# An attention and mixture-of-experts kernel on one core: the products with v of a half of the queries in one run, and their copies out of PSUM later in the order

## The chip, the cores and the metric

The kernel runs on one core of a Trainium2 chip. The metric is the device time of one launch in microseconds; lower is better. The core has five engines with an instruction stream each: TensorE (PE in the profile; PEld is its weight loads), VectorE (DVE), ScalarE (ACT), GpSimd (POOL) and SyncE (SP), which here only issues DMAs.

## The reference, cut to what matters

```python
scores = scale * np.matmul(q, k.transpose(0, 1, 3, 2))      # 8 batches, 8 heads, 576 x 64
scores = scores + bias.transpose(2, 0, 1)[None, :, :, :]    # a small MLP of the positions
scores = scores - np.max(scores, axis=-1, keepdims=True)
attn = np.exp(scores)
attn = attn / (np.sum(attn, axis=-1, keepdims=True) + 1e-09)
x = np.matmul(attn, v)                                      # then to tokens x 512
...
e_idx = np.argmax(x @ w_gate + modality_bias[modality_id], axis=1)
out[mask] = gate_w[mask, None] * (relu(x[mask] @ w1[e]) @ w2[e])   # for each of 8 experts
```

Everything is float32. The output has 4608 rows of 512.

## The kernel before

The program has three stages: a table of position biases, attention, and the experts. The change lies in attention, in the function `attention`.

Attention works on two heads of one batch at a time, a pair; there are 32 pairs, n = 0 to 31. The 576 queries of a pair come in five chunks (four of 128 for each head and a last one of 64 for both heads together), so a pair has nine score slots. A round of the outer loop over n has five steps u = 0 to 4, and the table `ORDER` says for each step, in letters, what is issued in which order. Every engine takes its own instructions in the order in which the letters issue them, so the table alone sets the order on each engine. The letters that matter:

- S: `scores`, four matmuls (line 420) into one of two score buffers `sps`; then VectorE adds the bias, takes the minimum and writes the chunk to `Eb` (line 435). e and f: ScalarE's exp (line 449) of the step's first and second score slot.
- t and T: `etrans`, four transposes of an exp chunk for head 0 and head 1 into PSUM, `eps[0]` for t and `eps[1]` for T (line 463), and a copy to `eT`. For the last chunk, in step u = 1, t is line 469 and T is the narrow transpose of line 474 (64 output columns for each head) into `eps[1]`, whose copy goes to `rT`. `take` is the copy out of PSUM; the list `ON_ACT` names those that ScalarE does (line 309), the others VectorE does. The transposes of chunk 3 of the round before (step 0) are both copied by ScalarE.
- R: `rtrans`, which transposes what is left of four chunks (line 491) into `rT`.
- a, A, b, c: `av`, the products with v of the pair before, n - 1. Half 0 of the queries is a and then A, half 1 is b and then c. Each letter is four narrow products (line 507, 64 output columns for each head, two heads side by side); A and c end with a product over all 128 columns (line 517). The float32 products are each run in two passes, so the profile counts eight for a letter. A and c then copy the sum out of PSUM to `xTb` on ScalarE (`av0`, `av1`).
- 0 to 4: `prep`, transposes of the next pair's q and k (lines 369 and 374) and their copies to `QT` and `KT`; there are prep steps for 30 of the rounds that have products.
- X and B are steps of the routing, W and K issue DMAs that swap halves of `QT` and gather `KH` and `QD` for the next pair's scores, C copies a remainder on GpSimd (line 454).

Three kinds of PSUM tile matter: `sps`, `eps`, and the two banks `xps`, handed out in turn by `xbank` to R, X, prep and the products. Whoever gets a bank waits until the copy out of its last use is done. In the listings, `xps_77` and `xps_78` are these two banks, `eps_751` and `eps_752` are `eps[0]` and `eps[1]`, `sps_749` and `sps_750` the two score buffers.

Of the kernel before, what the change touches and what calls it, by code (L numbers as in the profile page):

```python
# [22 lines left out]
S = 576  # L23
# [5 lines left out]
HS = S // 2  # L29
# [76 lines left out]
class Attn:  # L106
# [151 lines left out]
    def attn_early(self, st, rst):  # L258

        tc, nc, io = self.tc, self.nc, self.io  # L260
        pool = lambda **kw: st.enter_context(tc.tile_pool(**kw))
        cp = pool(name="ac", bufs=1)
        self.raw = pool(name="raw", bufs=2)
        self.Eb = cp.tile([P, 4, 2, S], F32, name="Eb")
        self.e_next = itertools.cycle(range(4))
        self.xrb = [cp.tile([P, XW], F32, name=f"xrb{k}") for k in range(2)]
        self.xr_next = itertools.cycle(self.xrb)
        right = lambda **kw: rst.enter_context(tc.tile_pool(side="right", **kw))

        last = (self.B - 1) % 2  # L270
        xp = {last: right(name="xtp_last", bufs=1), 1 - last: cp}
        self.xTb = [xp[k].tile([P, NP, S], F32, name=f"xTb{k}") for k in range(2)]
        self.smp = right(name="smp", bufs=2)
        self.rt = right(name="rt", bufs=1)

        self.idr = cp.tile([P, P], F32R, name="idr")
        nc.scalar.copy(self.idr, self.idf)
        self.eT = cp.tile([P, 2, 4, S], F32, name="eT")
        self.rT = cp.tile([P, S], F32, name="rT")
        self.qs = cp.tile([P, 9, 2, D], F32R, name="qs")  # L280
        self.ks = cp.tile([P, 9, 2, D], F32R, name="ks")
        self.KT = [cp.tile([P, 2, S], F32R, name=f"KT{k}") for k in range(2)]
        self.KH = cp.tile([P, S], F32R, name="KH")
        self.QD = cp.tile([P, P], F32R, name="QD")
        nc.gpsimd.memset(self.QD.bitcast(F32), 0.0)
        self.vrem = []
        for k in range(2):
            nc.vector.memset(self.QT[k][:, 0, 576:640].bitcast(F32), 0.0)
            vr = cp.tile([P, P], F32, name=f"vrem{k}")
            nc.vector.memset(vr, 0.0)  # L290
            self.vrem.append(vr)
        self.qraw, self.kraw, self.vmain, self.E, self.rem, self.sums, self.xT = {}, {}, {}, {}, {}, {}, {}

    def attn_late(self, st):

        pp = st.enter_context(self.tc.tile_pool(name="aps", bufs=1, space=PSUM))
        self.sps = [pp.tile([P, 2, 512], F32, name=f"sps{k}") for k in range(2)]
        self.eps = [pp.tile([P, 4, P], F32, name=f"eps{k}") for k in range(2)]
# [195 lines left out]
    def av(self, n, half, part):  # L494

        nc = self.nc
        if half == 0 and part == 0:
            self.xT[n] = self.xTb[n // NP % 2][:, n % NP, :]
        if part == 0:
            self.avps = self.xbank()  # L500
        v = self.vmain[n]
        sl = slice(HS * half, HS * half + HS)
        ps = self.avps[:, 0:HS]
        for k in (0, 1) if part == 0 else (2, 3):
            for h in range(2):
                o = slice(64 * h, 64 * h + 64)
                nc.tensor.matmul(  # L507
                    ps[o, :],
                    v[:, h, k, :],
                    self.eT[:, h, k, sl],  # L510
                    start=k == 0,
                    stop=False,
                    tile_position=(0, 64 * h),
                    skip_group_check=True,
                )
        if part == 1:
            nc.tensor.matmul(ps, self.vrem[n % 2], self.rT[:, sl], start=False, stop=True, skip_group_check=True)  # L517
        if part == 1:
            self.take(f"av{half}", self.xT[n][:, sl], ps)
            if half == 1:  # L520
                del self.vmain[n]

    def first_steps(self, route):

# [31 lines left out]


    ORDER = (
# [5 lines left out]
    )  # L564

    def attention(self):
        n_pair = self.n_pair
        tail = self.first_tiles() if self.K else {}
        for u, k in self.LATE:
            tail.setdefault((0, u), []).append(lambda k=k: next(self.late[k], None))  # L570
        bg = None
        for n in range(n_pair + 1):
            for u in range(5):
                for f in tail.get((n, u), ()):
                    f()
                if u == 4 and n > 0 and n % NP == 0:
                    assert not bg or all(k == len(x) for x, k in bg)
                    bg = self.route_steps(n // NP - 1)
                m, w = (n, u - 2) if u >= 2 else (n - 1, u + 3)
                scored = []  # L580
                for op in self.ORDER[u].split():
                    if op in "SefC":
                        if n == n_pair:
                            continue
                        if op == "S":
                            scored.append(self.scores(n, 2 * u + len(scored)))
                        elif op == "C":
                            self.compact(n, u)
                        else:
                            self.exps(*scored["ef".index(op)])  # L590
                    elif op in "tT":
                        if 0 <= m < n_pair:
                            self.etrans(m, w, "tT".index(op))
                    elif op in "RaAbc":
                        if n > 0:
                            self.rtrans(n - 1) if op == "R" else self.av(n - 1, *divmod("aAbc".index(op), 2))
                    elif op in "k01234WKV":
                        if n + 1 < n_pair:
                            if op in "01234":
                                self.prep(n + 1, int(op))()  # L600
                            else:
                                {"k": lambda: self.split(n + 1, 1), "W": lambda: self.swap(n + 1), "K": lambda: self.heads(n + 1), "V": lambda: self.load_v(n + 1)}[op]()
                    elif op in "qL":
                        if n + 2 < n_pair:
                            self.split(n + 2, 0) if op == "q" else self.load_qk(n + 2)
                    elif f := self.route_next(bg, "XB".index(op)):
                        f()
                if 0 <= m < n_pair:
                    del self.E[m, w]
        self.bg = bg  # L610
# [817 lines left out]
```

## Time and profile before

| what | value |
|---|---|
| median of three runs | 1195.97 us (1191.96 to 1196.64) |
| the profiled execution, its time | 1198.66 us |
| its span from the first to the last instruction | 1196.7 us |
| mean granted TensorE clock | 0.983 |
| TensorE matmul busy | 1132.1 us, 95% of the span |
| VectorE, ScalarE, GpSimd busy | 754.1, 728.3, 383.7 us (63%, 61%, 32%) |

All times below are of the profiled execution, which lies 2.7 us above the median of the runs. A row of the timeline has the start, the length from the start of its first to the end of its last instruction, the engine, line, operation, the tiles, and how many instructions it merges. A matmul's row ends after its results are out, so rows of neighbouring groups overlap; what a group costs TensorE is the distance from its start to the next group's start.

### The profile page before, as it was taken

Reading aid. Unit: us, or ns where it says so; the run is one execution under the profiler, and the core shown is the slowest. Engines: PE = TensorE matmul, PEld = TensorE weight load, DVE = VectorE, ACT = ScalarE, POOL = GpSimd, SP = SyncE. Lnnn points to the kernel's source line nnn. Section 1 sums busy time; section 2 is a strip of 40 time slices with the busy share of each in tenths; the row PEclk is TensorE's granted clock in tenths of the full one; section 3 lists DMA queues with packets and bytes.
Section 4 is the critical chain, followed back from the end, with each engine's and each line's share of the span. In section 5 each row is a group of like instructions: output and inputs, shape, how many; then the busy total and the mean of one; then the engine's idle time right before and its main releaser. Section 6 shows DMA issues by size and latency. Waiting matters only on the chain. (4 is left out here: it accounts for less than half of the span.)

```text
span 1196.7 us, 23090 instructions
## 1 busy us (share of the span) xinstructions
PE 1132.1 (95%) x8202; PEld 919.5 (77%) x8202; DVE 754.1 (63%) x1552; ACT 728.3 (61%) x1412; POOL 383.7 (32%) x525
## 2 busy tenths in 40 slices
PE   7977999899999899999998979999999999999997
PEld 3445777667778577777776758988899899989975
DVE  7974567457666475666757637577555645664667
ACT  5565667657767477677775654545545645554566
POOL 2203223434435325444353323532221123122122
PEclk9998999999999999999999999999999999999999
DMA  6854433764745635555365560221113314311361
GB/s 173 192 121 126 112 95 102 115 94 111 125 96 126 98 93 125 113 121 125 93 116 111 162 108 10 72 67 37 45 55 115 107 45 144 113 45 48 121 244 33
DMA packets 91311, 124.26 MB, mean 104 GB/s; under 512 B 35697, under 2 KB 60657, under 8 KB 91188
## 3 DMA queue, kind: packets, MB, share of 16 engines
q1 hardware_dynamic: 83188, 101.35, 36.3%
q0 software_dynamic: 8000, 21.35, 5.9%
q8 instruction: 68, 1.11, 0.5%
q14 instruction: 55, 0.45, 0.1%
HBM read 140.09 MB, written 19.90 MB: 134 GB/s over the span
## 5 line engine op out<-in xcount | busy, mean ns | idle before, releaser
L435 DVE CUSTOM_DVE_ANT_0 Eb<-sps,NBm 128x576 f32<-128x576 f32 x256 | 190.1, 755 | 183.8 <-PE sps L420 93.7
L449 ACT ACTIVATE Eb<-Eb,mn 128x576 f32<-128x576 f32 x288 | 221.5, 770 | 40.5 <-DVE mn L435 36.7
L420 PE MATMUL sps<-KT,QT 128*128 128x288 f32 x1152 | 222.7, 319 | 22.0 <-DMA QT<-QT 21.1
L420 PEld LDWEIGHTS sps<-KT,QT 128*128 128x128 f32 x1152 | 166.5, 191 | 27.4 <-issue 22.3
L1144 PE MATMUL p<-QT,w1hi 128*128 128x256 f32 x1152 | 163.9, 285 | 5.2 <-ACT w1hi L1117 5.2
L463 PE MATMUL eps<-idf,Eb 128*128 128x128 f32 x1024 | 159.9, 282 | 0.6 <-DVE lgs L781 0.3
L507 PE MATMUL xps<-eT,vraw 128*64 128x288 f32 x1024 | 155.0, 425 | 1.5 <-DVE QT L1129 1.0
L1144 PEld LDWEIGHTS p<-QT,w1hi 128*128 128x128 f32 x1152 | 150.8, 194 | 7.3 <-ACT w1hi L1117 6.1
L463 PEld LDWEIGHTS eps<-idf,Eb 128*128 128x128 f32 x1024 | 114.9, 142 | 39.5 <-issue 29.5
L1170 POOL DMA_INDIRECT out<-mo,idt x36 | 51.8, 1440 | 291.1 <-ACT mo L1169 262.6
L1147 DVE SCALAR_TENSOR_TENSOR hl<-p,hh 128x512 fp32r<-128x512 f32 x72 | 49.7, 690 | 138.9 <-ACT hh L1146 134.6
L454 POOL COPY rem<-Eb 128x128 f32<-128x128 f32 x128 | 37.5, 297 | 252.3 <-ACT Eb L449 245.1
L309 ACT ACTIVATE eT<-eps 128x512 f32<-128x512 f32 x192 | 111.4, 591 | 9.5 <-PE eps L463 8.7
L1161 PE MATMUL p<-w2lo,hh 128*128 128x512 f32 x288 | 112.9, 392 | 3.5 <-DVE w2lo L1111 2.2
L1111 DVE TENSOR_TENSOR w2lo<-NBm,w2hi 128x1024 fp32r<-128x1024 f32 x81 | 98.7, 1224 | 24.9 <-ACT w2hi L1110 24.8
L1161 PE MATMUL p<-w2hi,hh 128*128 128x512 f32 x288 | 114.0, 396 | 0.0
L1161 PE MATMUL p<-w2hi,hl 128*128 128x512 f32 x288 | 112.5, 391 | 0.0
L1146 ACT ACTIVATE hh<-p 128x512 fp32r<-128x512 f32 x72 | 43.1, 598 | 111.2 <-PE p L1144 103.1
L309 ACT ACTIVATE xTb<-xps 128x288 f32<-128x288 f32 x64 | 26.4, 412 | 122.9 <-PE xps L517 118.8
L507 PEld LDWEIGHTS xps<-eT,vraw 128*64 128x64 f32 x1024 | 63.1, 138 | 46.6 <-issue 12.6
L1111 DVE TENSOR_TENSOR w1lo<-NBm,w1hi 128x1024 fp32r<-128x1024 f32 x84 | 97.9, 1227 | 0.0
L1144 PE MATMUL p<-QT,w1lo 128*128 128x256 f32 x576 | 93.4, 285 | 0.3 <-DVE w1lo L1118 0.3
(227 smaller groups left out, 1991.3 us busy)
## 6 DMA issues: line engine op xcount, KB each, us to landing
NBm<-moe_w SPq DMA_DIRECT2D x24, 2048.0 KB
NBm<-moe_w SPq DMA_DIRECT2D x46, 1024.0 KB
QT<-QT SPq DMA_DIRECT2D x64, 304.0 KB
NBm<-xTb SPq DMA_DIRECT2D x32, 288.0 KB
KH<-KT SPq DMA_DIRECT2D x64, 144.0 KB
qraw<-q SPq DMA_DIRECT2D x32, 256.0 KB
kraw<-k SPq DMA_DIRECT2D x32, 256.0 KB
vraw<-v SPq DMA_DIRECT2D x32, 256.0 KB
```

The lines of the kernel that those rows point to most:

```text
L309: self.nc.scalar.activation(out, ps, AF.Copy, scale=scale)
L420: nc.tensor.matmul(ps[:, half, :], q, k[:, HS * half : HS * half + HS], start=i == 0, stop=i == len(terms) - 1, skip_group_check=True,)
L435: nc.vector.tensor_tensor_reduce(out=e.rearrange("p (t w) -> p t w", t=2), in0=ps, in1=nb.rearrange("p (t w) -> p t w", t=2), scale=1.0, s ...
L449: self.nc.scalar.activation(e, e, AF.Exp, bias=mn, scale=-1.0, accum_out=sm)
L463: nc.tensor.transpose(ps[:, k, :], e[:, part, P * k : P * k + P], self.idf)
L507: nc.tensor.matmul(ps[o, :], v[:, h, k, :], self.eT[:, h, k, sl], start=k == 0, stop=False, tile_position=(0, 64 * h), skip_group_check=True,)
L1111: (lo or self.nc.vector).tensor_tensor(l, w, h.bitcast(F32), op=ALU.subtract)
L1144: nc.tensor.matmul(ps[:, a, :], w[:, c, fs], x[:, c, :], start=i == 0, stop=i == len(ops) - 1)
L1146: nc.scalar.activation(hh[:, sl, :], ps, AF.Relu)
L1147: nc.vector.scalar_tensor_tensor(hl[:, sl, :], ps, 0.0, hh[:, sl, :].bitcast(F32), op0=ALU.max, op1=ALU.subtract)
L1161: nc.tensor.matmul(ps, h[:, f, sl], m[:, f, :], start=i == 0, stop=i == len(ops) - 1)
L1170: nc.gpsimd.indirect_dma_start(out=self.out, out_offset=IndirectOffsetOnAxis(ap=ids, axis=0), in_=o, in_offset=None, bounds_check=self.n_t ...
```

## The change

The four letters a, A, b, c move, two letters y and z are new, and the narrow transpose T of step 1 moves. The products of half 0 are issued as one run in step 1, directly behind the narrow transposes; those of half 1 as one run in step 3. The copies out of PSUM are split from the products (`av_out`, letters y and z) and are issued behind the step's second score and a transpose. Each half has its own entry in `avps`, so that the copy finds its bank.

```diff
+        self.avps = [None, None]
...
-            self.avps = self.xbank()
+            self.avps[half] = self.xbank()
...
-        if part == 1:
-            self.take(f"av{half}", self.xT[n][:, sl], ps)
-            if half == 1:
-                del self.vmain[n]
+
+    def av_out(self, n, half):
+        self.take(f"av{half}", self.xT[n][:, HS * half : HS * half + HS], self.avps[half][:, 0:HS])
+        if half == 1:
+            del self.vmain[n]
...
-        "S R S e f k X T a t B C",
-        "L S 1 A t e S 4 f 0 C T",
-        "t S S e f b q C T",
-        "B S c e S T 3 2 t f W C V",
+        "S R S e f k X T t B C",
+        "L S 1 T e a A S t y 4 f 0 C",
+        "t S S e f q C T",
+        "B S e b c S T z 3 2 t f W C V",
...
+                    elif op in "yz":
+                        if n > 0:
+                            self.av_out(n - 1, "yz".index(op))
```

The lines behind these shift by a few: 420 becomes 421, 463 becomes 464, 507 becomes 508, 309 becomes 310 and so on. A narrow group counted as x4 here is eight matmuls in the profile.

On TensorE, steps 0 and 1 of round 3, from the first products with v on, before:

```order
L507 MATMUL xps_78<-eT,vraw_1153 64x288 x4
L463 MATMUL eps_751<-idf,Eb 128x128 x4
L420 MATMUL sps_749<-KT_109,QT_73 128x288 x4
L369 MATMUL xps_77<-idr,qs 128x128 x4
L507 MATMUL xps_78<-eT,vraw_1153 64x288 x4
L517 MATMUL xps_78<-rT,vrem_114 128x288
L469 MATMUL eps_751<-idf,Eb 128x128 x4
L420 MATMUL sps_750<-KT_109,QT_73 128x288 x4
L374 MATMUL xps_78<-idr,qs 128x128
L374 MATMUL xps_78<-idr,ks 128x128
L369 MATMUL xps_77<-idr,qs 128x128 x4
L474 MATMUL eps_752<-idf,Eb 64x64 x2
```

and in the changed kernel, from the transposes T of step 0 on:

```order
L464 MATMUL eps_752<-idf,Eb 128x128 x4
L464 MATMUL eps_751<-idf,Eb 128x128 x4
L421 MATMUL sps_749<-KT_109,QT_73 128x288 x4
L370 MATMUL xps_78<-idr,qs 128x128 x4
L475 MATMUL eps_752<-idf,Eb 64x64 x2
L508 MATMUL xps_77<-eT,vraw_1153 64x288 x8
L518 MATMUL xps_77<-rT,vrem_114 128x288
L421 MATMUL sps_750<-KT_109,QT_73 128x288 x4
L470 MATMUL eps_751<-idf,Eb 128x128 x4
L375 MATMUL xps_78<-idr,qs 128x128
L375 MATMUL xps_78<-idr,ks 128x128
L370 MATMUL xps_77<-idr,qs 128x128 x4
```

The two groups of products of half 0 are one group of eight and stand right behind the narrow transposes (now 475), which have moved ahead of the second score; between the end of these products (518) and the transposes of q into the same bank `xps_77` stand a score group, four transposes and two more.

On TensorE, steps 2 and 3 of the same round, before:

```order
L420 MATMUL sps_749<-KT_109,QT_73 128x288 x4
L420 MATMUL sps_750<-KT_109,QT_73 128x288 x4
L507 MATMUL xps_78<-eT,vraw_1153 64x288 x4
L463 MATMUL eps_752<-idf,Eb 128x128 x4
L420 MATMUL sps_749<-KT_109,QT_73 128x288 x4
L507 MATMUL xps_78<-eT,vraw_1153 64x288 x4
L517 MATMUL xps_78<-rT,vrem_114 128x288
L420 MATMUL sps_750<-KT_109,QT_73 128x288 x4
L463 MATMUL eps_752<-idf,Eb 128x128 x4
L369 MATMUL xps_77<-idr,ks 128x128 x4
L369 MATMUL xps_78<-idr,ks 128x128 x4
```

and now:

```order
L421 MATMUL sps_749<-KT_109,QT_73 128x288 x4
L421 MATMUL sps_750<-KT_109,QT_73 128x288 x4
L464 MATMUL eps_752<-idf,Eb 128x128 x4
L421 MATMUL sps_749<-KT_109,QT_73 128x288 x4
L508 MATMUL xps_78<-eT,vraw_1153 64x288 x8
L518 MATMUL xps_78<-rT,vrem_114 128x288
L421 MATMUL sps_750<-KT_109,QT_73 128x288 x4
L464 MATMUL eps_752<-idf,Eb 128x128 x4
L370 MATMUL xps_77<-idr,ks 128x128 x4
L370 MATMUL xps_78<-idr,ks 128x128 x4
```

The products of half 1 are one group too. The bank that they write, `xps_78`, is wanted again by the last row, as before.

On ScalarE, steps 1 to 3 of the same round, before, from the copy of half 0 on (`xTb` is the copy out of the products, `KT` that of a prep step, `rT<-eps` that of the narrow transposes, `Eb` an exp):

```order
L309 ACTIVATE xTb_94<-xps_78 128x288
L309 ACTIVATE eT<-eps_751 128x4x2x64
L449 ACTIVATE Eb,sums_1377<-Eb,mn_2_1423 128x576
L309 ACTIVATE KT_108<-xps_78 128x2x64
L449 ACTIVATE Eb,sums_1377<-Eb,mn_3_1446 128x576
L309 ACTIVATE rT<-eps_752 128x64
L309 ACTIVATE eT<-eps_751 128x4x128
L449 ACTIVATE Eb,sums_1377<-Eb,mn_4_1472 128x576
L449 ACTIVATE Eb,sums_1377<-Eb,mn_5_1478 128x576
L309 ACTIVATE xTb_94<-xps_78 128x288
L449 ACTIVATE Eb,sums_1377<-Eb,mn_6_1499 128x576
L309 ACTIVATE eT<-eps_752 128x4x128
```

and now:

```order
L310 ACTIVATE rT<-eps_752 128x64
L450 ACTIVATE Eb,sums_1377<-Eb,mn_2_1419 128x576
L310 ACTIVATE eT<-eps_751 128x4x2x64
L310 ACTIVATE xTb_94<-xps_77 128x288
L310 ACTIVATE KT_108<-xps_78 128x2x64
L450 ACTIVATE Eb,sums_1377<-Eb,mn_3_1443 128x576
L310 ACTIVATE eT<-eps_751 128x4x128
L450 ACTIVATE Eb,sums_1377<-Eb,mn_4_1472 128x576
L450 ACTIVATE Eb,sums_1377<-Eb,mn_5_1478 128x576
L450 ACTIVATE Eb,sums_1377<-Eb,mn_6_1495 128x576
L310 ACTIVATE eT<-eps_752 128x4x128
L310 ACTIVATE xTb_94<-xps_78 128x288
```

The copy `xTb` of half 0 stood ahead of the copy `eT` of step 1 and an exp, and now stands behind both; that of half 1 stood ahead of an exp and the copy `eT` of step 3, and now stands behind both.

More of the change, by code (lines that the diff above doesn't have):

```diff
@@ L499, in av @@
         if part == 0:
-            self.avps = self.xbank()
+            self.avps[half] = self.xbank()
         v = self.vmain[n]
         sl = slice(HS * half, HS * half + HS)
-        ps = self.avps[:, 0:HS]
+        ps = self.avps[half][:, 0:HS]
         for k in (0, 1) if part == 0 else (2, 3):
```

## The prediction

> **What bounds the kernel now.** I read the page first, then a table of stretches (the span cut at the start and the end of the rounds that hold products, and one undisturbed round), then who waits for whom, then the timeline of TensorE and of ScalarE in that round.
>
> ```profile
> PE 1132.1 (95%) x8202; PEld 919.5 (77%) x8202; DVE 754.1 (63%) x1552; ACT 728.3 (61%) x1412; POOL 383.7 (32%) x525
> ...
> 98.26:712.36 614.10, 592.60 (x4569) 461.65 (x4569) 380.76 (x1021) 411.64 (x979) 236.56 (x382) 0.98 0.53 112
> 468.31:486.83 18.52, 18.52 (x146) 14.02 (x145) 11.57 (x31) 13.06 (x33) 9.58 (x15) 1.00 0.67 128
> ```
>
> The columns of the last two rows are the stretch, its length, and the busy time of TensorE, weight loads, VectorE, ScalarE and GpSimd, then the clock. In the undisturbed round TensorE is busy for all of its 18.52 us; ScalarE has 5.5 us free, VectorE 7. So whatever shortens TensorE's row of groups shortens the round, and whatever makes TensorE wait for another engine lengthens it, as long as the others keep up. In the whole stretch TensorE waits for 21.5 us, most of it outside the change:
>
> ```profile
> PE sps L420 <- DMA QT<-QT: 21.1, 4, 13.9
> ...
> PE xps L374 <- POOL ks L356: 4.2, 2, 3.0
> ...
> PE xps L491 <- POOL rem L454: 3.6, 1, 3.6
> ```
>
> (The 13.9 us are before the stretch.) Here is TensorE's row of groups in the undisturbed round, from T of step 0 to t of step 3:
>
> ```profile
> 469.27 0.60 PE L463 MATMUL eps<-idf,Eb 128*128 128x128 f32 x4
> 469.80 1.19 PE L507 MATMUL xps<-eT,vraw 128*64 128x288 f32 x8
> 470.92 0.66 PE L463 MATMUL eps<-idf,Eb 128*128 128x128 f32 x4
> 471.33 0.78 PE L420 MATMUL sps<-KT,QT 128*128 128x288 f32 x4
> 471.95 0.45 PE L369 MATMUL xps<-idr,qs 128*128 128x128 f32 x4
> 472.33 1.19 PE L507 MATMUL xps<-eT,vraw 128*64 128x288 f32 x8
> 473.45 0.75 PE L517 MATMUL xps<-rT,vrem 128*128 128x288 f32 x2
> 474.04 0.60 PE L469 MATMUL eps<-idf,Eb 128*128 128x128 f32 x4
> 474.39 0.78 PE L420 MATMUL sps<-KT,QT 128*128 128x288 f32 x4
> 475.01 0.22 PE L374 MATMUL xps<-idr,qs 128*128 128x128 f32 x1
> ...
> 475.13 0.50 PE L369 MATMUL xps<-idr,qs 128*128 128x128 f32 x4
> 475.56 0.34 PE L474 MATMUL eps<-idf,Eb 128*64 128x64 f32 x4
> 475.83 0.66 PE L463 MATMUL eps<-idf,Eb 128*128 128x128 f32 x4
> 476.24 1.30 PE L420 MATMUL sps<-KT,QT 128*128 128x288 f32 x8
> 477.47 1.19 PE L507 MATMUL xps<-eT,vraw 128*64 128x288 f32 x8
> 478.59 0.66 PE L463 MATMUL eps<-idf,Eb 128*128 128x128 f32 x4
> 479.01 0.77 PE L420 MATMUL sps<-KT,QT 128*128 128x288 f32 x4
> 479.71 1.19 PE L507 MATMUL xps<-eT,vraw 128*64 128x288 f32 x8
> 480.83 0.75 PE L517 MATMUL xps<-rT,vrem 128*128 128x288 f32 x2
> 481.21 0.91 PE L420 MATMUL sps<-KT,QT 128*128 128x288 f32 x4
> 481.95 0.60 PE L463 MATMUL eps<-idf,Eb 128*128 128x128 f32 x4
> 482.31 0.89 PE L369 MATMUL xps<-idr,ks 128*128 128x128 f32 x8
> 483.02 0.63 PE L463 MATMUL eps<-idf,Eb 128*128 128x128 f32 x4
> ```
>
> And ScalarE in the same round, with one row of the weight loads and one of VectorE:
>
> ```profile
> 470.10 0.39 PEld L507 LDWEIGHTS xps<-eT,vraw 128*64 128x64 f32 x4
> ...
> 470.33 0.78 ACT L449 ACTIVATE Eb<-Eb,mn 128x576 f32<-128x576 f32 x1
> ...
> 471.11 1.11 ACT L309 ACTIVATE eT<-eps 128x512 f32<-128x512 f32 x2
> ...
> 473.45 0.30 PEld L517 LDWEIGHTS xps<-rT,vrem 128*128 128x128 f32 x2 [0.44 <-issue]
> ...
> 474.24 0.41 ACT L309 ACTIVATE xTb<-xps 128x288 f32<-128x288 f32 x1 [2.02 <-PE xps L517]
> ...
> 474.68 0.60 ACT L309 ACTIVATE eT<-eps 128x512 f32<-128x512 f32 x1
> ...
> 477.15 0.76 DVE L435 CUSTOM_DVE_ANT_0 Eb<-sps,NBm 128x576 f32<-128x576 f32 x1 [0.37 <-issue]
> ...
> 482.69 0.59 ACT L309 ACTIVATE eT<-eps 128x512 f32<-128x512 f32 x1
> ...
> 483.23 0.60 ACT L309 ACTIVATE KT<-xps 128x512 fp32r<-128x512 f32 x1
> ```
>
> **What the change takes from TensorE.** No matmul goes or comes; what goes is borders between narrow and full-width groups (the 0.44 us in which the weight loads stand still at 473.45 is part of one). A run of eight narrow matmuls costs 1.12 us with its borders (469.80 to 470.92). Inside it, the last four loads, 0.14 us each (page: 138 ns), take 0.39 us, so two side-by-side matmuls follow the last two after 0.25 us, a little less without the step between the heads; I take 0.24. Sixteen in one run then cost 1.12 + 4 x 0.24 = 2.08 us in place of 2.24, and the groups beside them lose their own borders.
>
> First stretch, T of step 0 to t of step 2: 475.83 - 469.27 = 6.56 us before. After: T 0.44 and t 0.36 (transposes as at 481.95, 0.36, and one more step of 0.08 between two such groups), scores 0.62, prep 0.38, narrow transposes 0.20, products 2.08, line 517 0.38 (as at 480.83), scores behind it 0.74 (as at 481.21), t 0.36, then 0.20 for the two and 0.36 for the four prep transposes (eight take 0.71 at 482.31). The sum is 6.12: 0.44 us less.
>
> Second stretch, scores of step 2 to the second score of step 3: 481.21 - 476.24 = 4.97 before. After: eight scores 1.15 (0.62 for four, and the x8 row is 0.52 longer than an x4 row), T 0.36, scores 0.70, products 2.08, line 517 0.38, in all 4.67: 0.30 less. Together 0.74 us a round; 32 runs of products: **24 us less**.
>
> The trace has no narrow transposes directly ahead of narrow products. If that border were free, the group would cost 0.11 (two steps of its own); if it cost as leaving and entering do now, 0.27 (475.56 to 475.83) and some 0.1 more: 0.2 is nearer to what stays in one shape; the ends are 3 us less and 5 us more over all rounds. [...]
>
> **What the change makes TensorE wait for.** Three places, in the same round's times.
>
> T of step 1 writes `eps[1]`, which holds chunk 3's transposes until ScalarE has copied them. That copy stands behind the exp of step 0's second score (470.33), which nothing in the change moves: the pair of copies begins at 471.11, the first is out at about 471.70 (591 ns on the page). The new row reaches T at 469.27 + 0.44 + 0.36 + 0.62 + 0.38 = 471.07. Wait: **0.63 us**. Behind it stand all products. Rounds with a step X have one more copy ahead of it on ScalarE and four more transposes on TensorE, which nearly cancel. Before, T came 4.5 us later and nothing waited.
>
> Prep 0 takes the bank that half 0's products filled. ScalarE copies it only behind `eT` of step 1, which itself needs t. From the first transpose of t, the row at 474.04 is finished 0.60 later, the copy starts 0.04 after that (474.68), the next copy follows 0.54 after a first (482.69 to 483.23) and takes 0.41: the bank is free 1.59 us after t began. TensorE is at prep 0 after 0.36 + 0.20 = 0.56. Wait: 1.03, with about 0.02 for the signal **1.05 us**. Behind it stand t and all of step 2. Before, the copy went first (474.24 to 474.65) and its bank was asked for at 475.01.
>
> Prep 2 takes the bank of half 1 in the same way: T, `eT` and the copy end 1.59 after T began; T and prep 3 take 0.36 + 0.36 = 0.72. Wait: **0.88 us**.
>
> A small one: step 3's first score needs the buffer that VectorE empties in 0.76 us (477.15). With step 2 shortened by one run of products it comes about **0.1 us** early.
>
> The exp moved ahead on ScalarE gains nothing, since ScalarE had 2.02 us free there (474.24) and does not set the end. GpSimd and SP keep their order; the swap's DMAs depend on prep 0's copy, which comes 1.2 us later, while the round grows by more.
>
> **The sum.** 30 rounds x (1.05 + 0.88) = 57.9; 31 x (0.63 + 0.1) = 22.6; less 24: +56.5 us. Against that, some waits that are there now shrink when TensorE comes later: those in the first fence but for the 13.9, 15 us (7.2 + 4.2 + 3.6), and some half-speed clock behind the long ones. They hang on DMAs and on GpSimd's own pace, and each round leaves them 0.6 to 1.9 us more. Bounds 0 and 15; I take 9. Result +47: 1198.66 + 47 = 1246 for a profiled execution, and 2.7 less, **1243 us**, for the median.
>
> **Rivals.**
> 1. Faster. The waits do not bind, only the borders go: 1196 - 24 = 1172. [...] It decides if ScalarE has emptied a half's bank within 0.56 us of t's start, against 1.59 by the rows. That needs the copy ahead of `eT`, and the listing has it behind. [...]
> 2. Smaller loss: the wait at T is hidden (23 us less) or the old waits go whole (6 less), about 1220.
> 3. Larger loss: prep 0 and 2 come so late that the swap and the gather reach the next pair's scores late more often; the three such waits of the first fence now cost 7.2 us together, up to 3 each, and one in every second round at 1.5 us gives 22 more: about 1265.
> 4. A wash, if the waits are half of what I count: within 6 us of before.
>
> **Chances.** Forecast (1228 to 1256) 0.70; smaller loss 0.12; larger 0.11; faster 0.04; wash 0.03. The range 1216 to 1264 leaves out the faster and the wash cases and the outer part of the rest. About 0.5% is what a measurement of this kernel can tell: slower by more than that 0.93, within it 0.03, faster 0.04.
>
> **What would show it.** Right: in the changed trace TensorE waits on ScalarE at the narrow transposes, at the four prep 0 transposes and at prep 2's, some 30 times each, of 0.6, 1.0 and 0.9 us; a plain round is 20.2 to 20.6 us long; TensorE's busy share in attention falls to about 88%; the two runs of products start eight narrow passes 0.24 us apart. Wrong: no wait at the prep transposes, or copies of the products that start ahead of `eT`'s end. The prediction fails if the borders are worth much more than 0.74 us a round, or the bank is free earlier than the row of copies says.

## The result, and the profile after

The changed kernel is slower: 1253.53 us median against 1194.47 for the kernel before on the same chip, a ratio of 1.0498 (95% interval 1.0467 to 1.0528), so 59 us more where 47 were forecast (range 1216 to 1264). The profiled execution of the changed kernel took 1256.16 us, its span 1254.2.

The stretches of the changed kernel: all rounds with products, then the four rounds of one batch; ahead of them the same four rounds of the kernel before (the third, 18.52 us, is the undisturbed round of the prediction). Columns as in the prediction, with the share of the DMA engines' time and the GB/s that they moved at the end.

```profile
430.49:449.61 19.12, 18.79 (x149) 14.78 (x148) 14.82 (x47) 13.98 (x35) 5.48 (x11) 1.00 0.35 90
449.61:468.31 18.70, 18.70 (x151) 15.20 (x150) 10.77 (x25) 13.58 (x32) 10.41 (x15) 1.00 0.63 142
...
486.83:505.17 18.34, 18.34 (x151) 14.59 (x150) 11.50 (x30) 12.38 (x31) 6.98 (x14) 1.00 0.43 103
```

```profile
98.40:769.75 671.35, 586.63 (x4568) 469.37 (x4566) 380.05 (x1021) 413.54 (x979) 237.03 (x382) 0.99 0.47 103
...
459.91:481.85 21.94, 18.92 (x148) 15.08 (x147) 14.91 (x47) 14.19 (x35) 5.50 (x11) 1.00 0.31 79
481.85:502.60 20.75, 18.54 (x151) 15.46 (x150) 10.80 (x25) 13.68 (x32) 10.41 (x15) 1.00 0.51 128
502.60:523.14 20.54, 18.37 (x147) 14.28 (x146) 11.53 (x31) 13.12 (x33) 9.31 (x15) 1.00 0.64 118
523.14:543.11 19.97, 18.21 (x152) 14.80 (x151) 11.37 (x29) 12.36 (x31) 7.21 (x15) 1.00 0.41 91
```

A round that kept TensorE busy throughout now has two microseconds in which it does nothing: 20.54 us with 18.37 busy, in place of 18.52 with 18.52. TensorE's busy share of the stretch fell from 96% to 87%, while its busy time fell by only 6 us, though the saved borders are worth about 25 (below): the profile counts a part of each new wait, in which the last results still come out, as busy. In the plain round the four waits come to 2.82 us (below), and TensorE's idle time to 2.17. The other engines' busy times are nearly the same, so nothing became a new bound by its load. Who waited for whom on TensorE:

```profile
PE xps L370 <- ACT xTb L310: 45.3, 58, 0.9
PE eps L475 <- ACT eT L310: 19.6, 29, 1.1
```

These are the three places of the forecast with its counts: the prep transposes (two places in a round, 58 times in all) behind the copy `xTb` of the products, and the narrow transposes behind the copy `eT`. The plain round, TensorE and then ScalarE, with one row of VectorE at the end:

```profile
504.97 0.45 PE L370 MATMUL xps<-idr,qs 128*128 128x128 f32 x4
506.03 0.34 PE L475 MATMUL eps<-idf,Eb 128*64 128x64 f32 x4 [0.61 <-ACT eT L310]
506.19 2.11 PE L508 MATMUL xps<-eT,vraw 128*64 128x288 f32 x16
508.24 0.75 PE L518 MATMUL xps<-rT,vrem 128*128 128x288 f32 x2
...
509.36 0.60 PE L470 MATMUL eps<-idf,Eb 128*128 128x128 f32 x4
509.71 0.30 PE L375 MATMUL xps<-idr,qs 128*128 128x128 f32 x1
509.85 0.23 PE L375 MATMUL xps<-idr,ks 128*128 128x128 f32 x1
510.94 0.54 PE L370 MATMUL xps<-idr,qs 128*128 128x128 f32 x4 [0.86 <-ACT xTb L310]
...
512.84 0.60 PE L464 MATMUL eps<-idf,Eb 128*128 128x128 f32 x4
513.43 0.80 PE L421 MATMUL sps<-KT,QT 128*128 128x288 f32 x4
...
517.73 0.54 PE L370 MATMUL xps<-idr,ks 128*128 128x128 f32 x4
518.97 0.28 PE L370 MATMUL xps<-idr,ks 128*128 128x128 f32 x1 [0.70 <-ACT xTb L310]
```

```profile
505.40 1.06 ACT L310 ACTIVATE eT<-eps 128x512 f32<-128x512 f32 x2
...
509.99 0.60 ACT L310 ACTIVATE eT<-eps 128x512 f32<-128x512 f32 x1 [2.60 <-PE eps L470]
510.49 0.41 ACT L310 ACTIVATE xTb<-xps 128x288 f32<-128x288 f32 x1
...
518.01 0.60 ACT L310 ACTIVATE eT<-eps 128x512 f32<-128x512 f32 x1 [1.72 <-PE eps L464]
518.51 0.41 ACT L310 ACTIVATE xTb<-xps 128x288 f32<-128x288 f32 x1
...
512.61 0.76 DVE L436 CUSTOM_DVE_ANT_0 Eb<-sps,NBm 128x576 f32<-128x576 f32 x1 [0.33 <-POOL rem L455]
```

At 506.03 the narrow transposes start 0.05 us after the first copy of the pair at 505.40 is out (0.58 long, to 505.98). At 509.99 ScalarE, which had stood idle for 2.60 us, copies `eT` first; the products' copy ends at 510.90, and the prep transposes begin 0.04 later. TensorE's second half of the round repeats this: the copy at 518.51 ends at 518.92, and the transposes begin at 518.97. The number in brackets counts from the end of the last result; from the moment TensorE could have gone on, the waits are 0.68 (506.03 less 504.97 and 0.38), 1.03 (510.94 less 509.71 and 0.20) and 0.88 us (518.97 less 517.73 and 0.36). A fourth wait shows no bracket: the score at 513.43 starts 0.59 us behind the transposes at 512.84, which alone take 0.36; VectorE's row at 512.61 reads its buffer until 513.37.

### The profile page after: what moved, and what is told of

It is laid out like the page before. It is cut to its first block, busy times and chain, and to the rows that moved or that the text cites. A ratio compares the mean times of both kernels' runs of the same rounds, so it can differ in the third digit from the quotient of the medians.

```text
span 1254.2 us, 23070 instructions
## 1 busy us (share of the span) xinstructions
PE 1125.0 (90%) x8202; PEld 927.0 (74%) x8202; DVE 753.7 (60%) x1552; ACT 729.8 (58%) x1412; POOL 386.3 (31%) x525
## 4 chain that ended last, share of the span: by engine, by line
PE 54%; DMA 13%; issue 11%; ACT 9%; DVE 6%; POOL 5%; SPq 3%; POOLq 0%; ACTq 0%; DVEq 0%
PE p L1149 12%; PE p L1166 12%; PE xps L508 7%; PE sps L421 7%; PE eps L464 4%; ACT Eb L450 4%; PE bps L187 3%; DMA NBr<-xg,idt 3%; DMA qraw<-q 3%; PE xps L518 2%; ACT eT L310 2%; PE xps L370 2%; DMA xg<-xrb 2%; DMA QT<-QT 2%; ACT xTb L310 1%
## 5 line engine op out<-in xcount | busy, mean ns | idle before, releaser
L421 PE MATMUL sps<-KT,QT 128*128 128x288 f32 x1152 | 227.8, 324 | 22.9 <-DMA QT<-QT 16.9
L421 PEld LDWEIGHTS sps<-KT,QT 128*128 128x128 f32 x1152 | 169.2, 192 | 39.7 <-issue 17.8
L464 PE MATMUL eps<-idf,Eb 128*128 128x128 f32 x1024 | 149.5, 277 | 1.2 <-ACT eT L310 0.7
L508 PE MATMUL xps<-eT,vraw 128*64 128x288 f32 x1024 | 139.1, 415 | 0.7 <-issue 0.7
L464 PEld LDWEIGHTS eps<-idf,Eb 128*128 128x128 f32 x1024 | 117.5, 142 | 9.6 <-DVE mn L436 5.0
L508 PEld LDWEIGHTS xps<-eT,vraw 128*64 128x64 f32 x1024 | 69.0, 139 | 45.2 <-issue 7.9
L1116 DVE TENSOR_TENSOR w1lo<-NBm,w1hi 128x1024 fp32r<-128x1024 f32 x84 | 97.9, 1228 | 0.3 <-ACT w1hi L1115 0.3
L1115 ACT CAST w2hi<-NBm 128x1024 fp32r<-128x1024 f32 x84 | 86.8, 1041 | 0.9 <-PEq L1280 0.9
```

What stands on the lines that cost most here:

```text
L421: nc.tensor.matmul(ps[:, half, :], q, k[:, HS * half : HS * half + HS], start=i == 0, stop=i == len(terms) - 1, skip_group_check=True,)
L464: nc.tensor.transpose(ps[:, k, :], e[:, part, P * k : P * k + P], self.idf)
L508: nc.tensor.matmul(ps[o, :], v[:, h, k, :], self.eT[:, h, k, sl], start=k == 0, stop=False, tile_position=(0, 64 * h), skip_group_check=True,)
L1115: self.nc.scalar.copy(h, w)
L1116: (lo or self.nc.vector).tensor_tensor(l, w, h.bitcast(F32), op=ALU.subtract)
```

## The experiments

Each is given as the change of `ORDER` (the lines with a minus say of which kernel), and as a ratio to the kernel before, run on the same chip. Where two profiles are compared, they can be from different chips. The changed kernel itself ran once more, on a second chip:

> The changed kernel as it is, beside these on one chip. All theories: ratio to before 1.045 to 1.053, as the first time.

Measured: 1265.18 us against 1205.08, ratio 1.0498 (1.0462 to 1.0534), as on the first chip.

Theory: the time lies in TensorE's waits for ScalarE's copies. Rivals: the long narrow runs themselves, or the moved narrow transposes alone.

**Copies directly behind the products.**

```diff
-        "L S 1 T e a A S t y 4 f 0 C",
+        "L S 1 T e a A y S t 4 f 0 C",
-        "B S e b c S T z 3 2 t f W C V",
+        "B S e b c z S T 3 2 t f W C V",
```

> The changed kernel with both copies of the products issued directly behind the products, ahead of the score and the transpose; the merged runs and the early narrow transposes stay. Theory (TensorE waits for the bank at prep 0 and prep 2): those two waits go, 30 x (1.05 + 0.88) = 58 us, some 5 us of the old waits on DMAs and GpSimd come back: about 1200 us (1195 to 1206); a plain round 18.6 us in place of 20.5; the wait at the narrow transposes stays at 0.6 to 1.0 us, 30 times. Rival (the merged runs or the moved narrow transposes are what costs): 1240 or more, and TensorE still stands 40 us elsewhere.

Measured: ratio 1.0125 (1.0078 to 1.0173). Three quarters of the loss went with the place of the two copies, and the waits at prep with it; the narrow transposes still wait (21.2 us in 28 waits). So the rival is out as the main cost. But the kernel is some 9 us above the forecast, outside its range, and its plain round is 19.01 us, not 18.6. One wait is new, the first transposes of step 2 behind `eT`; and step 3's first score waits as in the changed kernel:

```profile
564.60 0.34 PE L475 MATMUL eps<-idf,Eb 128*64 128x64 f32 x4 [0.61 <-ACT eT L310]
...
569.22 0.66 PE L464 MATMUL eps<-idf,Eb 128*128 128x128 f32 x4 [0.22 <-ACT eT L310]
...
570.78 0.60 PE L464 MATMUL eps<-idf,Eb 128*128 128x128 f32 x4
571.36 0.80 PE L421 MATMUL sps<-KT,QT 128*128 128x288 f32 x4
```

**Narrow transposes back at the end of step 1**, copies late.

```diff
-        "L S 1 T e a A S t y 4 f 0 C",
+        "L S 1 e a A S t y 4 f 0 C T",
```

> The changed kernel with the narrow transposes back at the end of step 1, the merged runs and the late copies kept. Theory: the wait at the narrow transposes goes (31 x 0.65, in one round of four 1.0: 22 us), their own two borders come back (about 0.25 us a round, 8 us), the waits at prep 0 and prep 2 stay: about 1239 us (1232 to 1245). Rival (the early narrow transposes are the main cost): below 1215.

Measured: ratio 1.0342 (1.0293 to 1.0392), 41 us above before (by this chip's times; 44 were expected). The waits at prep are what they were (45.7 us in 59). So the narrow transposes' early place costs about 19 us of the 60, net of the border that it saves, and the late copies most of the rest.

**The copies moved alone**, products in four runs as before.

```diff
-        "L S 1 A t e S 4 f 0 C T",
+        "L S 1 A t e S y 4 f 0 C T",
-        "B S c e S T 3 2 t f W C V",
+        "B S c e S T z 3 2 t f W C V",
```

> The kernel before with only the copies moved: the products stay in four runs, the copy of half 0 is issued behind t, the exp and the second score, that of half 1 behind the score and T. Theory: prep 4 now waits for half 0's bank, which is free after eT, an exp and the copy, about 1.4 us later than asked for, and prep 2 waits 0.88 us: 30 x 2.3 = 68 us, less up to 10 of old waits: about 1257 us (1245 to 1265). Rival (late copies cost nothing by themselves, only with the merged runs): 1195 us.

Measured: ratio 1.0447 (1.0395 to 1.0499), 51 us, where some 62 were expected. Late copies cost this much without any merged run:

```profile
PE xps L375 <- ACT xTb L310: 36.4, 30, 1.2
PE xps L370 <- ACT xTb L310: 20.8, 30, 0.7
```

**Everything that gains, nothing that waits?** The narrow transposes stand between the two halves of the run.

```diff
-        "L S 1 T e a A S t y 4 f 0 C",
+        "L S 1 e a T A y S t 4 f 0 C",
-        "B S e b c S T z 3 2 t f W C V",
+        "B S e b c z S T 3 2 t f W C V",
```

> The merged runs with the copies directly behind the products, and the narrow transposes between the first and the second half of the products of half 0, so that their PSUM tile has one microsecond more to come free. Theory: no new wait but 0.2 us at step 3's first score; the borders gain 0.74 us a round, 24 us, less 6 for that score and up to 5 of old waits that grow: about 1179 us (1172 to 1186), ratio to before 0.98 to 0.993. Rival (fewer borders gain nothing, TensorE meets another wait): 1192 or more.

Measured: ratio 1.0028 (1.0003 to 1.0053). A miss: no gain. The borders are gone, yet a plain round takes 18.32 us:

```profile
550.34:568.66 18.32, 18.10 (x146) 14.22 (x145) 11.43 (x31) 13.28 (x33) 9.56 (x15) 1.00 0.62 133
```

```profile
557.70 0.66 PE L464 MATMUL eps<-idf,Eb 128*128 128x128 f32 x4 [0.22 <-ACT eT L310]
558.12 1.31 PE L421 MATMUL sps<-KT,QT 128*128 128x288 f32 x8
559.26 0.60 PE L464 MATMUL eps<-idf,Eb 128*128 128x128 f32 x4
559.85 0.79 PE L421 MATMUL sps<-KT,QT 128*128 128x288 f32 x4
```

The groups that moved away had filled two latencies. The transposes at 557.70 now follow so soon that `eT` of step 1 is not out: between the two transposes stood a score and the narrow transposes. And from T at 559.26 to the score at 559.85 it takes 0.59 us where T alone takes 0.36, since the score's buffer is not empty: VectorE's row at 559.02 takes 0.76 us and reads it until 559.78. Before, the first products of half 1 stood ahead of T. The second shows in the changed kernel as well (512.84 to 513.43 is 0.59). The first does not: there the prep transposes wait for a copy that comes after `eT`, and step 2's transposes follow them without a wait.

**One score ahead of those transposes.** The kernel of the last run, with

```diff
-        "t S S e f q C T",
+        "S t S e f q C T",
```

> The run before it (narrow transposes inside the merged run, copies directly behind the products), with step 2's first score moved ahead of its first transposes: S t S in place of t S S. That run's plain round lost 0.22 us to those transposes, which waited for ScalarE's copy of step 1's, and 0.23 us to step 3's first score, which waited for VectorE. Theory (the moved products had covered these two waits, and the saved borders went there): both go, since the score fills the first and reaches VectorE 0.4 us earlier; a plain round takes 17.8 to 17.95 us in place of 18.33, 30 x 0.45 = 13 us, of which up to 6 are lost to old waits on DMAs and GpSimd that grow: ratio to before 0.985 to 0.996. Rival (the saved borders never existed): a plain round of 18.3 us and a ratio of 1.00 or more.

> The same kernel as the run with step 2's score ahead, beside the one with the earlier loads on one chip: ratio to before 0.990 to 0.997, as the first time.

Measured: ratio 0.9935 (0.9906 to 0.9964), and in the repetition on another chip 0.9979 (0.9958 to 1.0000), outside what was expected of it. The round has no wait, and is a little shorter than forecast (17.8 to 17.95):

```profile
542.52:560.23 17.71, 17.71 (x146) 14.21 (x145) 11.44 (x31) 12.60 (x30) 7.31 (x10) 1.00 0.69 132
```

So the borders are worth 18.52 - 17.71 = 0.81 us a round. Of the 25 us that this makes over 31 rounds, 2.5 to 8 us arrive. The profile shows more of the waits on other chains:

```profile
PE sps L421 <- DMA QT<-QT: 24.8, 9, 14.0
PE p L1149 <- DVE w1lo L1123: 11.8, 2, 11.0
PE xps L375 <- POOL ks L357: 10.8, 4, 6.2
PE xps L492 <- POOL rem L455: 5.2, 5, 2.1
```

Scores wait 10.8 us for the swap of `QT` (beside the first 14.0), where it was 7.2; GpSimd's `ks` 10.8, where it was 4.2; and the expert stage starts with one wait of 11.0 for a part of an expert's weights (`w1lo`), where it was 5.2 for another part. That profile of the kernel before is from another chip. The first kernel of the next experiment ran on this one, with plain rounds of 18.51 us: beside it, from the start of the first of the rounds to the start of the last, TensorE is busy 21 us less (583.1 to 562.1) but stands idle 13 us more (23.1 to 36.1), and what follows takes 3.6 us more. So the borders do leave TensorE's row of groups, and most of what they free is spent waiting.

**One half alone**, half 1 in one run, without and with that score ahead.

```diff
-        "t S S e f b q C T",
-        "B S c e S T 3 2 t f W C V",
+        "t S S e f q C T",            # the second kernel: S t S
+        "B S e b c z S T 3 2 t f W C V",
```

> The kernel before with the products of half 1 in one run in step 3 and nothing else moved (its copy directly behind, as before). Theory: two borders go, 0.30 us a round, and step 3's first score waits 0.2 to 0.25 us for VectorE, since the products of step 2 no longer stand between: ratio 0.996 to 1.003. Rival (borders count in full): 0.992 or less.

> The same with S t S in step 2. Theory: the wait of the first score of step 3 goes, the border gain of 0.30 us a round shows: 9 us less, up to 3 of them lost to old waits: ratio 0.991 to 0.997, a plain round of 18.2 to 18.3 us in place of 18.5. Rival: no better than without it.

Measured: 1.0019 (0.9993 to 1.0045) and 0.9994 (0.9966 to 1.0023). The rounds, without and with the score ahead:

```profile
469.97:488.48 18.51, 18.51 (x147) 14.17 (x145) 11.48 (x31) 13.33 (x33) 8.31 (x13) 1.00 0.72 130
```

```profile
544.75:563.07 18.32, 18.32 (x146) 14.18 (x145) 11.56 (x31) 13.22 (x33) 9.56 (x15) 1.00 0.65 132
```

Without it the round is where it was (18.52): the border gain of half 1 is spent on the score's wait, as expected (0.56 us from T at 479.10 to the score at 479.66). With it the round is 0.20 shorter, less than the 0.30 counted: the two scores of step 2 are no longer one group, and take 0.65 and 0.62 us (552.27 to 552.92, 553.27 to 553.89) where 1.15 was counted for both. The total shows nothing: its forecast missed.

**Where the gain goes.** Each batch has five scatters on GpSimd. Before the change, 13 of their waits, 46.5 us in all, are for an earlier scatter to land, and `ks` and `rem` come behind them on the same engine: the `rem` for which TensorE waited 3.56 us starts at 410.49, as the scatter of 409.56 ends, and that one had waited 3.18 us for a DMA. These two kernels leave four of the five out, and the row loads of the first tiles of the expert stage skip the numbers that are then missing; most rows of the output are not computed:

```diff
                 n = P if c < 4 else 64
+                if c > 0:
+                    return
                 nc.gpsimd.indirect_dma_start(out=self.tab, ...)
...
                 in_offset=IndirectOffsetOnAxis(ap=self.idt[t % 6][:, w : w + 1], axis=0),
+                bounds_check=n - 1,
+                oob_is_err=False,
```

```profile
POOL tab L857 <- DMA tab<-ids,pos: 46.5, 13, 7.8
```

> The kernel before with four of the five indirect scatters of every batch left out (most token numbers never reach the table, so most rows of the output are not computed from their tokens; the first tiles' row loads skip numbers out of bounds). On GpSimd each scatter waits for the one before to land. Theory (that chain of scatters is what takes back time once TensorE is faster): the waits of TensorE on GpSimd's ks and rem go, and part of those on DMAs: 5 to 15 us below before, ratio 0.987 to 0.996. Rival (the waits come from DMA traffic alone): ratio 0.998 or more.

> The kernel with the narrow transposes inside the run and step 2's score ahead, with the same scatters left out. Theory: the border gain of 0.8 us a round now reaches the total, 20 to 25 us below the kernel before with the same scatters left out, where it was 6 us with all scatters: ratio to before 0.968 to 0.980, and the expert stage begins without the 11 us wait for VectorE's w1lo. Rival (swap DMAs or the weights take it back): less than 12 us between the two.

Measured: 0.9787 (0.9753 to 0.9821) and 0.9691 (0.9657 to 0.9724), 1177.64 and 1167.25 us. Without four of the five scatters the kernel before is 26 us faster, more than expected; TensorE's waits on `ks` and `rem` are gone, and the longest wait at the start of the expert stage is down to 0.8. In the profiles the rounds, first start to last, are 19.5 us shorter (601.8 to 582.3): TensorE stands idle 11.7 us less (20.0 to 8.3), and is busy 7.8 us less with the same matmuls. The second part goes with the clock, which in these rounds of the kernel before dropped to 0.50 behind four waits of 2.06, 2.98, 3.22 and 3.56 us, for 3.4 us each (6.8 behind the 2.98), beside the one at their start: after the one of 3.56 us, a run of eight narrow matmuls takes 2.19 us in place of 1.19:

```profile
410.84 0.33 PE L491 MATMUL xps<-idf,rem 128*128 128x128 f32 x1 [3.56 <-POOL rem L454]
...
412.80 2.19 PE L507 MATMUL xps<-eT,vraw 128*64 128x288 f32 x8
...
411.00:416.00 5.00, 5.00 (x32) 3.07 (x32) 0.90 (x3) 2.84 (x7) 2.62 (x6) 0.66 0.56 119
```

(The last row is a stretch; its clock is 0.66, and 0.50 from 412.1 to 415.5.) The mean granted clock of the runs, 0.981 for the kernel before on this chip, is 0.9895 without the scatters. About 14.6 of the 19.5 us are gained by the start of the 26th of these rounds (at 579.8 us in the kernel before), ahead of the first row load (at 669.9), so the skipped rows are not the main cause. Whether it is the waits from scatter to scatter or the time that the scatters themselves take (GpSimd is busy 25 us less in the rounds) was not separated.

Between the two kernels lie 10.4 us, not the 20 to 25 of the theory, and within what the rival allowed. TensorE is busy 17.4 us less in the rounds and idle 7.0 us more. What is left on TensorE is the swap of `QT` (19.8 us with the first 12.9, against 17.6 with 14.0) and smaller gains in the other rounds of a batch. So the scatters are at most a part of the answer to where the gain goes: 10.4 of 25 us arrive in place of 2.5 to 8, and the interval of the 8 (4 to 11 us) reaches as far. The rounds show the rest: the plain round keeps its 0.8 us, but the first round of a batch gains only 0.3 (19.12 to 18.82), and in the batch shown the second gives it back (18.79 to 19.23, with 1.04 us in which TensorE does nothing), in part to a wait of 0.87 us for the swap; the first rounds are alike in the other batches, the second ones range from 0.6 shorter to 0.9 longer. The first three rounds of one batch in the second kernel, and that wait:

```profile
407.29:426.11 18.82, 18.39 (x149) 14.90 (x148) 14.94 (x47) 14.15 (x35) 5.44 (x11) 1.00 0.36 91
426.11:445.34 19.23, 18.19 (x150) 15.41 (x149) 10.81 (x25) 14.53 (x34) 10.07 (x16) 1.00 0.59 138
445.34:463.06 17.72, 17.72 (x147) 14.21 (x146) 11.44 (x31) 12.60 (x30) 5.92 (x11) 1.00 0.54 137
...
445.00 0.51 PE L421 MATMUL sps<-KT,QT 128*128 128x288 f32 x2 [0.87 <-DMA QT<-QT]
```

Why the first round gains so little stays open; there VectorE is busiest (14.94 of the 18.82 us).

**Loads of q and k earlier**, in the kernel with the score ahead: `L` moves from step 1 to the front of step 0.

> The run with step 2's score ahead, all scatters kept, and the loads of q and k for the pair after next issued at the start of step 0 instead of step 1, so that fewer bytes stand ahead of the swap of QT. Theory (part of the saved time is lost to the swap's DMAs, 10.8 us of waits of scores on QT beside the 14.0 at the start): those waits fall to 5 us or less, the scatter waits stay: ratio to before 0.985 to 0.992. Rival (the swap waits for something else, or GpSimd's chain takes what is freed): 0.993 or more, like the run before it.

Measured: ratio 0.9876 (0.9842 to 0.9910), the fastest of all with every part computed, while the same kernel without it was at 0.9979 beside it. The time is as the theory had it, but the cause is not shown: the waits on `QT` were to fall from 10.8 us to 5 or less, and the profiled execution, the slowest of its runs (1203.92 us against a median of 1190.64), has 15.8 us of them beside the first 14.0, one of them 8.4.

## Why the prediction held, step by step

- Borders, 0.74 us a round: 0.81 with every wait gone, and the sum of a plain round then closes: 0.68 + 1.03 + 0.88 + 0.23 - 0.81 = 2.01 us longer, measured 20.54 - 18.52 = 2.02. The sixteen narrow passes took 2.05 us (506.19 to 508.24), forecast 2.08. The unknown border between narrow transposes and narrow products is nearly free: the group takes 0.16 us (506.03 to 506.19), of which 0.11 are its own two steps. With the narrow transposes inside the run of products, the fourth change above, it takes 0.12 (554.11 to 554.23).
- The waits: 0.63, 1.05 and 0.88 forecast for a plain round, 0.68, 1.03 and 0.88 measured. Of the 1.05, 0.02 for the signal from the copy to TensorE was the author's estimate, which no run shows; the transposes start 0.04 and 0.05 us after the copies end (510.90 and 518.92). The copies moved alone show the same waits without the merged runs (36.4 and 20.8 us).
- The small term was mis-sized: the first score of step 3, 0.1 us in the forecast, is 0.59 - 0.36 = 0.23, 4 us more over 31 rounds.
- The step that was too small is taking one plain round for all. The first round of a batch grew by 2.82 us (19.12 to 21.94). There VectorE does routing work ahead of the scores (three instructions of 0.2 us from 460.85 on, its score row at 461.42), which delays the exp (1.08 us of waiting, below) and `eT`: the narrow transposes wait 1.10 us (464.38 less 462.90 and 0.38), 0.42 more than in the plain round. And the score behind the transposes of step 0 has a wait of its own, for VectorE to empty its buffer: it starts 1.16 us behind two groups that take 0.80 elsewhere (503.56 to 504.36), since the products that stood between them are gone and VectorE reads that buffer until 462.18. With these two the round's waits, less the borders, come to 2.79:

```profile
461.08 1.06 PE L464 MATMUL eps<-idf,Eb 128*128 128x128 f32 x8
462.24 0.81 PE L421 MATMUL sps<-KT,QT 128*128 128x288 f32 x4
...
464.38 0.34 PE L475 MATMUL eps<-idf,Eb 128*64 128x64 f32 x4 [1.02 <-ACT eT L310]
...
462.22 0.78 ACT L450 ACTIVATE Eb<-Eb,mn 128x576 f32<-128x576 f32 x1 [1.08 <-DVE mn L436]
```

The four rounds of the batch grew by (83.2 - 74.7) / 4 = 2.13 us on average, where the sum gives 56.5 / 31 = 1.82. Over 31 rounds that is 9.5 us, most of the 12 by which the forecast was low; 1253.5 us lies near the upper end of the forecast of 1228 to 1256.
- The old waits were to give back 9 us. 31 x 2.13 = 66, and the time from the first round's start to the last one's grew by 58 (601.8 to 660.2): some 8 came back, if all batches are like this one. Read from the waits themselves, the 15.0 us of the first fence fell to 8.6 (2.9 on `QT`, 1.5 on `ks`, 4.2 on `rem`).
- The rivals: faster by the borders alone is wrong by what stands around them; with the waits avoided, the full border gain is in the plain round, but 0.2 to 0.65% in the total. The smaller loss and the wash did not come, since all three waits were there in full. Nor did the larger loss by late swaps: the scores waited 2.9 us for `QT` beside the first 14.0, less than the 7.2 before.

## What to carry to other kernels

Before a group of work is moved out of an engine's row, look at what stood behind it: it may be the cover of a latency on another engine, here a copy out of PSUM and a reduction (0.22 and 0.23 us a round), and the gain of a saved border is paid back there. A copy that frees a buffer belongs ahead of copies that nobody waits for (two such copies moved back took the ratio from 1.0498 to 1.0125), and how late it may come is counted from who asks next for that buffer, not from who reads the copy. A gain measured in one undisturbed round need not reach the total: here, when the round had lost all its own waits, more than half of what it saved appeared as waits on DMAs and on other engines.

## What the runs showed that was not expected

GpSimd's scatters, which looked like a few stray waits of TensorE (4.2 and 3.6 us), cost far more: with four of five left out the kernel before falls from 1203.37 to 1177.64 us. A part of that is the matmul clock: behind the wait of 3.56 us it ran at a granted 0.50 for 3.4 us, so that this wait cost some 1.7 us more than its own length (an estimate, half of the 3.4). And the same program differed by 0.9% between chips (1194.47 and 1205.08 us for the kernel before), so the times are compared as ratios taken on one chip.
